# Short convolution and channel mix on one core: a rebuilt opening (weight softmax over eight partitions, mixing coefficients turned on TensorE, band matrices by thirds, load order) and a tail kept pair by pair

## The chip, the core and the metric

One core of a Trainium2 chip runs the program. Its engines work side by side and meet by semaphores: TensorE (PE; its weight loads are listed as PEld), VectorE (DVE), ScalarE (ACT), GpSimd (POOL), and SyncE (SP), which only issues transfers. PE writes to PSUM, which the kernel uses as a ring of four tiles of two banks; ACT and DVE read it. Transfers are issued by SP, ACT or POOL, and those from POOL convert fp32 to bf16 on the way. The metric is the device time of one execution in microseconds (us).

## The reference

Eight sequences of 4160 positions with 192 channels. First a causal convolution with seven taps, the taps of each of eight heads (24 channels each) being a softmax over raw weights; then a channel mix with a token shift.

```python
w = np.exp(weight - weight.max(-1, keepdims=True))      # weight: (8 heads, 7 taps)
w = w / (w.sum(-1, keepdims=True) + 1e-09)
y[b, s, h, :] = sum(w[h, k] * x_pad[b, s + k, h, :] for k in range(7))   # x_pad: 6 zeros ahead
y_prev = y one position earlier, zeros at the start
yk = mu_k * y + (1 - mu_k) * y_prev
yr = mu_r * y + (1 - mu_r) * y_prev
k = np.maximum(yk @ w_k, 0)                              # 192 -> 1024
out = 1 / (1 + np.exp(-(yr @ w_r))) * (k * k @ w_v)      # 1024 -> 192
```

## The kernel before

Two sequences are worked on together (four pairs). The tokens of a pair go through steps of 512 (256 for the first), and each step's 192-to-1024 product falls into slots of one PSUM tile; four slots are a bundle. Every slot needs six or twelve matmuls with the weights `wk`, one ReLU on ACT and one square on DVE; the product with `wv` follows some bundles later. The convolution is a matmul with a 128x128 banded matrix per head (`toe`), made once at the start. For the first eleven blocks of 120 positions (groups 0, 1 and 2 with 3, 4 and 4 blocks) it is done so that the result comes out with channels on partitions (`conv_t`); later groups go through DRAM.

The opening, which the change rebuilds, and the first bundle:

```python
    def softmax():
        nc.vector.tensor_reduce(out=w_max, in_=w_raw, axis=mybir.AxisListType.X, op=ALU.max)
        nc.vector.tensor_tensor(
            out=w_exp, in0=w_raw, in1=w_max.unsqueeze(2).to_broadcast([1, H, K]), op=ALU.subtract
        )
        nc.scalar.activation(out=w_exp, in_=w_exp, func=AF.Exp)
        nc.scalar.activation(out=w_sig, in_=w_exp[:, 0, 0:1], func=AF.Sigmoid)
        xbs[0] = three.tile([P, GB, 2, D], BF16, tag="xb", name="xb")
        for s in range(2):
            nc.scalar.copy(out=xbs[0][:, : groups[0][2], s, :], in_=x_f32[:, :, s, :])
        # then DVE: sum, reciprocal, product -> w_nrm [1, H, K]; PE: ones.T @ w_nrm -> w_bc on 128 partitions
    # ... cut ...
    def make_toe():   # for heads 0-5, then heads 6-7: w_bc * mod8 -> w_all, summed -> w_per (tap by position mod 8),
                      # then toe = w_per * band        (three DVE instructions each)
    # ... cut ...
    def prologue():
        nc.sync.dma_start(out=w_raw, ...)
        nc.vector.memset(x_f32[0:32, 0, :, :], 0.0)
        nc.vector.memset(ones_t, 1.0)
        for st in range(2):
            load_x_first(nc.scalar, 0, P, 1, groups[0][2], st, st + 1)
        load_x_first(nc.sync, 16, P, 0, 1, 0, 2)
        load_mu(0, moe_mu_k)
        load_x_first(nc.scalar, HALO, 16, 0, 1, 0, 2)
        nc.scalar.preload_act_table(AF.Exp)
        nc.vector.memset(zeros, 0.0)
        x_tile(1)
        load_x(1)
        # POOL: affine_select -> ident
        masks_band()
        load_wk()
        for i in range(SHORT):                 # 100 matmuls of one column
    # ... cut ...
        warm(warm_ps, WARM[0])
        x_tile(2)
        masks_mod8()
        softmax()
        warm(warm_ps, WARM[1])
        make_toe()
        load_x(2)
        load_mu(1, moe_mu_r)
        x_tile(3)
        load_x(3)
        load_wr()
        load_wv()
        x_tile(4)
        load_x(4)

    def bundle_first(ns):
        new_yT(0)
        tiles = [ring.tile([P, 2, BANK], FP32, tag="k", name="ps_t") for _ in range(2)]
        for n, (g, c) in enumerate((g, c) for g in range(2) for c in range(NC)):
            o = tiles[n % 2][:, n // 2 % 2, :]
            conv_t(g, c, o, range(groups[g][2]))
            to_yT(g, c, o, 0, groups[g][2], nc.scalar.copy)
            if g == 0:
                diff(0, slice(c, c + 1))
                mix(0, 0, slice(c, c + 1))
        for c in range(NC):
            for n in ns[:2]:
                k_mm(n, (c,))
        for n in ns[:2]:
            k_relu(n)
        for c in range(NC):
            diff(1, slice(c, c + 1))
            mix(1, 0, slice(c, c + 1))
        for n in ns[2:]:
            k_mm(n)
            k_relu(n)
        for n in ns:
            k_square(n)
```

`conv_t` of one channel third, the slot product and the mixing. `mu` holds the mixing coefficients with the channel on the partition:

```python
    def conv_t(g, c, o, blocks):               # both sequences of every block: 8 matmuls of 120 columns a block
    # ... cut ...
                        nc.tensor.matmul(
                            out=o[p0 : p0 + m, n * BLK : (n + 1) * BLK],
                            lhsT=xbs[g][:, i, s, c0 : c0 + m],
                            rhs=toe[:, h, 0:BLK], start=True, stop=True)
    def k_mm(n, cs=range(NC)):                 # wk columns of slots 0, 1 of step 0: first half; slots 2, 3: second half
    # ... cut ...
                    nc.tensor.matmul(out=ps[:, i, f * L : (f + 1) * L], lhsT=wk[r, c, fs], rhs=xk[r, c, :L], ...)
    def mix(s, i, sl=slice(0, NC)):            # step 0: one instruction a third; later: scale() and add_y()
    # ... cut ...
            nc.vector.scalar_tensor_tensor(out=t[:, c, :L], in0=d[:, c, :L], scalar=mu[:, i, c : c + 1],
                in1=y_of(s, sl, 0)[:, 0, :], op0=ALU.mult, op1=ALU.add)
```

From the third bundle on (`b` counts from 0), `mix_a`, `mix_b` and `mix_c` hold the mixing work that is due, `quad` is a product with `wv`, and `tr` turns group 3:

```python
    def bundle_rest(b, ns):
    # ... cut ...
        k_mm(ns[0])
        k_relu(ns[0])
        k_square(ns[0])
        if b > 2:
            run(mix_b, b)
            conv_half(units[0], 0)
        k_mm(ns[1])
        if b > 2:
            conv_half(units[0], 1)
        k_relu(ns[1])
        if b > 2:
            k_square(ns[1])
        run(rq, b)
        if quad:
            v_rows(*quad, 0)
        if b == 2:
            tr(3, 0)
            tr(3, 1)
            k_square(ns[1])
            run(mix_b, b)
        k_mm(ns[2])
        k_relu(ns[2])
        if b == 2:
            conv_half(units[0], 0)
    # ... cut ...
```

The last 64 positions of all eight sequences make one step of 256 tokens at the end; `keep_tail` stores their convolution results, and `v_last` writes the four results of 128 tokens:

```python
    y_tail = const.tile([P, NC, NPAIR // 2, TAIL + 1, 2], BF16)
    def keep_tail(p):
        c0 = YC + T0 - 1
        nc.gpsimd.tensor_copy(out=y_tail[:, :, p // 2, :, p % 2], in_=yTs[p][:, :, c0 : c0 + TAIL + 1])
    # ... cut ...
    def v_last(s, j):
    # ... cut ...
        for k in range(4):
            ps = ring.tile([P, 2, BANK], FP32, tag="k", name="ps_v")
            v_mm(ps[:, 0, 0:D], s, tile_of(s, j, k))
            nc.vector.tensor_tensor(
                out=o_sb[:, k, :],
                in0=ps[:, 0, 0:D],
                in1=r_sb[:, k // 2, k % 2 * D : (k % 2 + 1) * D],
                op=ALU.mult,
            )
            # one transfer of 128 rows for each k, by SP for k = 0, 2 and by ACT for k = 1, 3
```

## Time and profile before

| What | Value |
|---|---|
| time, median of three runs | 417.99 us (417.91 to 418.95) |
| span of the profiled execution | 416.2 us |
| PE busy | 407.2 us (98%) |
| DVE busy | 378.8 us (91%) |
| ACT busy | 347.7 us (84%) |
| POOL busy | 48.9 us (12%) |
| bytes moved by DMA | 64.59 MB, mean 155 GB/s |

Busy time is the union of an engine's instructions; a matmul's end is modelled, so a busy PE need not stream all the time. In a line of instruction groups, the columns are line and engine, operation, tiles and shapes, count, then busy us and mean ns of one, then the idle time of the engine ahead of them and what ended it. The chain of waits follows the end of the program back to whatever released each step.

### The profile page before, as it was taken

How to read it: one execution, taken by the hardware profiler on the slowest of the kernel's cores; microseconds unless marked ns; L12 is line 12 of the kernel's file. 1: busy time of each engine (PE TensorE's matmuls, PEld its weight loads, DVE VectorE, ACT ScalarE, POOL GpSimd, SP SyncE). 2: the span in 40 equal slices, each digit the busy share in tenths (PEclk: the TensorE clock that was granted, in tenths of full speed). 3: DMA queues.
4: the chain of work that ended last, by engine and by line, in shares of the span. 5: the costliest groups of instructions: out<-in, count | busy, mean ns of one | idle time of the engine just before them, and what ended most of it. 6: DMA issues, size and time to landing. Idle time of an engine off the chain costs nothing.

```text
span 416.2 us, 16358 instructions
## 1 busy us (share of the span) xinstructions
PE 407.2 (98%) x7136; PEld 316.0 (76%) x7136; DVE 378.8 (91%) x674; ACT 347.7 (84%) x408; POOL 48.9 (12%) x73
## 2 busy tenths in 40 slices
PE   6999999999999999999999999999999999999996
PEld 3667777787887778778777877877777787777895
DVE  5898799999999999999999999999999999999974
ACT  5999898898888889888988888898898788777781
POOL 6650003102030100202012010201000000000000
PEclk9999999999999999999999999999999999999999
DMA  9999779958499794959689693897936564421223
GB/s 144 193 191 178 191 185 196 224 148 160 122 196 227 166 182 120 151 164 186 175 149 204 181 183 109 146 225 148 181 95 162 139 152 125 119 69 49 77 80 115
DMA packets 134682, 64.59 MB, mean 155 GB/s; under 512 B 84926, under 2 KB 134610, under 8 KB 134610
## 3 DMA queue, kind: packets, MB, share of 16 engines
q1 hardware_dynamic: 95876, 48.28, 45.2%
q0 software_dynamic: 37872, 14.66, 30.9%
q8 instruction: 56, 0.92, 0.9%
q10 hardware_dynamic: 862, 0.61, 0.5%
q14 instruction: 16, 0.13, 0.1%
HBM read 29.89 MB, written 36.99 MB: 161 GB/s over the span
## 4 chain that ended last, share of the span: by engine, by line
PE 92%; ACT 3%; DVE 3%; issue 1%; POOL 0%; ACTq 0%; POOLq 0%
PE ps_v L577 40%; PE ps_k L492 38%; PE ps_r L549 7%; PE ps_c L310 5%; ACT k_sb L504 2%; PE ps_v L532 1%; DVE k L518 1%; ACT y L356 1%; PE warm L702 1%; DVE d L435 0%; POOL xb L126 0%; ACT yT L340 0%; DVE xk L448 0%; DVE xk L472 0%; DVE xk L466 0%
## 5 line engine op out<-in xcount | busy, mean ns | idle before, releaser
L504 ACT ACTIVATE k_sb<-ps_k 128x1024 bf16<-128x1024 f32 x260 | 260.9, 1039 | 53.2 <-PE ps_k L492 53.1
L492 PE MATMUL ps_k<-xk,wk 64*128 64x512 bf16 (+1 forms) x1632 | 200.3, 367 | 0.8 <-ACT k_sb L504 0.3
L518 DVE TENSOR_TENSOR k<-k_sb 128x1024 bf16<-128x1024 bf16 x260 | 177.7, 688 | 14.5 <-ACT k_sb L504 7.4
L577 PE MATMUL ps_v<-wv,k 64*128 64x192 bf16 x4032 | 188.8, 243 | 0.7 <-ACT k_sb L504 0.2
L577 PEld LDWEIGHTS <-k 64*128 64x128 bf16 x4032 | 172.4, 94 | 13.9 <-issue 1.5
L492 PEld LDWEIGHTS <-wk 64*128 64x128 bf16 x1632 | 87.9, 94 | 51.4 <-issue 1.1
L593 DVE TENSOR_TENSOR o_sb<-ps_v,r_sb 128x768 f32<-128x768 f32 x64 | 61.2, 957 | 11.1 <-PE ps_v L577 4.5
L557 ACT ACTIVATE r_sb<-ps_r 128x768 bf16<-128x768 f32 x65 | 54.6, 842 | 0.0
L126 POOL DMA_DIRECT2D xb<-in_x_dram x34 | 30.6, 903 | 193.1 <-PE ps_c L310 93.0
L356 ACT CAST y<-ps_c 120x960 bf16<-120x960 f32 (+4 forms) x67 | 50.7, 787 | 2.2 <-PE ps_c L310 2.1
L549 PEld LDWEIGHTS <-xr 64*128 64x128 bf16 x780 | 36.1, 94 | 11.0 <-issue 0.4
L549 PE MATMUL ps_r<-wr,xr 64*128 64x192 bf16 x780 | 43.8, 243 | 0.0
L310 PE MATMUL ps_c<-xb,toe 64*128 64x480 bf16 (+2 forms) x240 | 39.2, 335 | 0.3
L466 DVE TENSOR_SCALAR xr<-d,mu 128x512 bf16<-128x512 bf16 (+1 forms) x102 | 35.9, 355 | 0.0
L466 DVE TENSOR_SCALAR xk<-d,mu 128x512 bf16<-128x512 bf16 (+1 forms) x99 | 33.0, 361 | 0.1
L435 DVE TENSOR_TENSOR d<-yT 128x1536 bf16<-128x1536 bf16 (+3 forms) x37 | 31.3, 847 | 0.9 <-ACT yT L340 0.9
L472 DVE TENSOR_TENSOR xr<-xr,yT 128x1536 bf16<-128x1536 bf16 (+1 forms) x33 | 31.0, 938 | 1.1
L472 DVE TENSOR_TENSOR xk<-xk,yT 128x1536 bf16<-128x1536 bf16 (+2 forms) x34 | 30.5, 898 | 0.1
L310 PEld LDWEIGHTS <-toe 64*128 64x128 bf16 x240 | 13.4, 94 | 11.8 <-issue 0.9
L419 POOL COPY y_tail<-yT 128x195 bf16<-128x195 bf16 x4 | 1.7, 429 | 68.7 <-DMA yT<-y_dram 68.7
L108 POOL MEMSET xb<- 32x384 bf16 x3 | 1.2, 408 | 45.1 <-PE ps_k L492 43.8
L330 PEld LDWEIGHTS <-xb 128*32 128x32 bf16 (+3 forms) x264 | 4.3, 101 | 2.6 <-issue 1.6
(52 smaller groups left out, 61.9 us busy)
## 6 DMA issues: line engine op xcount, KB each, us to landing
out_dram<-o_sb SPq DMA_DIRECT2D x128, 192.0 KB, 2.8
y_dram<-y SPq DMA_DIRECT2D x10, 900.0 KB, 6.5
xb<-in_x_dram POOLq DMA_DIRECT2D x14, 480.0 KB, 7.9
xb<-in_x_dram POOLq DMA_DIRECT2D x6, 432.0 KB, 8.0
xb<-in_x_dram POOLq DMA_DIRECT2D x10, 192.0 KB, 5.1
y_dram<-y SPq DMA_DIRECT2D x3, 450.0 KB, 5.3
y_dram<-y SPq DMA_DIRECT2D x1, 810.0 KB, 6.0
wk<-in_moe_w_k_dram POOLq DMA_DIRECT2D x4, 192.0 KB, 6.7
```

The lines of the kernel that those rows point to most:

```text
L310: nc.tensor.matmul(out=banks[:, bank, :, :, k * G : (k + 1) * G], lhsT=toe[q, h, :], rhs=xbs[g][q, :nb, :, h * G : (h + 1) * G], start=hal ...
L356: copy(out=bass.AP(tensor=y.tensor, offset=y.offset + d0, ap=[y.ap[0], [d1 - d0, 2], [2 * D, nb], [Q, 2], [1, n]],), in_=bass.AP(tensor=ps ...
L435: nc.vector.tensor_tensor(out=shaped(s, diffs[s][:, cs, :L]), in0=y_of(s, cs, 1), in1=y_of(s, cs, 0), op=ALU.subtract)
L466: nc.vector.tensor_scalar(out=t[:, c, :L], in0=diffs[s][:, c, :L], scalar1=mu[:, i, c : c + 1], scalar2=None, op0=ALU.mult)
L472: nc.vector.tensor_tensor(out=o, in0=o, in1=y_of(s, sl, 0), op=ALU.add)
L492: nc.tensor.matmul(out=ps[:, i, f * L : (f + 1) * L], lhsT=wk[r, c, fs], rhs=xk[r, c, :L], start=c == 0 and f == 0, stop=c == NC - 1 and f ...
L504: nc.scalar.activation(out=k_sb, in_=ps.rearrange("p a b -> p (a b)"), func=AF.Relu)
L518: nc.vector.tensor_tensor(out=o, in0=i, in1=i, op=ALU.mult)
L549: nc.tensor.matmul(out=ps[:, i, k * D : (k + 1) * D], lhsT=xr[q, c, ts], rhs=wr[q, c, :], start=c == 0, stop=c == NC - 1,)
L557: nc.scalar.activation(out=r_sbs[s, j], in_=ps[:, :, 0 : 2 * D], func=AF.Sigmoid)
L577: nc.tensor.matmul(out=v_ps[s, j][:, bank, k * D : (k + 1) * D], lhsT=k2s[s][q, f, t * P : (t + 1) * P], rhs=wv[q, f, :], start=half == 0 ...
L593: nc.vector.tensor_tensor(out=o_sb.rearrange("p (b t) d -> p b (t d)", b=2), in0=v_ps.pop((s, j)), in1=r_sbs.pop((s, j)), op=ALU.mult,)
```

## The change

The opening is rebuilt so that the band matrices are there sooner. The eight heads of the softmax lie on eight partitions instead of one; Exp takes the negated maximum as its bias and gives the sum as well. Normalised weights are turned by a 32x32 DVE transpose, and eight small matmuls with shifted selection matrices (`tap8`) leave `w_per` in PSUM, in place of broadcast, mask and sum. `toe` is made in three parts, one for each third of the channels, and the copy of the first x goes by thirds too. The mixing coefficients are loaded as six rows and turned by a PE transpose, instead of a scatter of single elements. The first half of `wk` is asked for ahead of group 1 of x. In the third bundle the mixing and a square are issued ahead of the transposes. The tail is kept pair by pair instead of interleaved by two pairs, and is written by eight transfers instead of four.

```diff
-    WARM = (3, 5)
-    SHORT = 100
+    WARM = (3, 2)
+    SHORT = 95
     def load_mu(i, m):
-        for st in range(2):
-            nc.sync.dma_start(
-                out=mu[st * Q : (st + 1) * Q, i, :], in_=bass.AP(tensor=m.tensor, offset=m.offset, ap=[[1, Q], [Q, NC]])
-            )
+        nc.sync.dma_start(
+            out=mu_raw[i * NC : (i + 1) * NC, :].rearrange("c (s q) -> c s q", s=2),
+            in_=bass.AP(tensor=m.tensor, offset=m.offset, ap=[[Q, NC], [0, 2], [1, Q]]),
+        )
-    w_all = place[:, n : n + H * 8 * K].rearrange("p (h r k) -> p h r k", h=H, r=8)
-    w_raw = const.tile([1, H, K], FP32)
+    w_raw = const.tile([H, K], FP32)
-    w_nrm = const.tile([1, H, K], BF16)
-    mod8 = const.tile([P, 16], FP32)
+    w_nrm = const.tile([32, 32], BF16)
+    w_tap = const.tile([32, 32], BF16)
+    tap8 = const.tile([8, P + 8], BF16)
+    ident6 = const.tile([2 * NC, 2 * NC], FP32)
+    mu_raw = const.tile([2 * NC, P], FP32)
-    w_bc = ring.tile([P, 2, BANK], FP32, tag="k", name="w_bc")[:, 0, 0 : H * K].rearrange("p (h k) -> p h k", h=H)
-    w_per = const.tile([P, H, 8], BF16)
+    w_ps = ring.tile([P, 2, BANK], FP32, tag="k", name="w_ps")
+    w_per = w_ps[:, 0, 0 : H * 8].rearrange("p (h r) -> p h r", r=8)
-    y_tail = const.tile([P, NC, NPAIR // 2, TAIL + 1, 2], BF16)
+    y_tail = const.tile([P, NC, NPAIR, TAIL + 2], BF16)
@@ softmax, masks @@
-        nc.vector.tensor_reduce(out=w_max, in_=w_raw, axis=mybir.AxisListType.X, op=ALU.max)
-        nc.vector.tensor_tensor(
-        # ... exp of the difference, a Sigmoid on one element, copies by sequence, sum, reciprocal, product ...
+        nc.vector.tensor_reduce(out=w_max, in_=w_raw, axis=mybir.AxisListType.X, op=ALU.max, negate=True)
+        nc.scalar.activation(out=w_exp, in_=w_raw, func=AF.Exp, bias=w_max, accum_out=w_sum)
+        nc.scalar.preload_act_table(AF.Sigmoid)
         xbs[0] = three.tile([P, GB, 2, D], BF16, tag="xb", name="xb")
-        for s in range(2):
-            nc.scalar.copy(out=xbs[0][:, : groups[0][2], s, :], in_=x_f32[:, :, s, :])
-        nc.vector.tensor_reduce(out=w_sum, in_=w_exp, axis=mybir.AxisListType.X, op=ALU.add)
+        for c in range(NC):
+            cs = slice(c * Q, (c + 1) * Q)
+            nc.scalar.copy(out=xbs[0][:, : groups[0][2], :, cs], in_=x_f32[:, :, :, cs])
         nc.vector.reciprocal(out=w_sum, in_=w_sum)
-        # ... product, matmul of ones with w_nrm -> w_bc; masks_mod8: two DVE reductions of ident ...
+        nc.vector.tensor_scalar(
+            out=w_nrm[0:H, 0:K], in0=w_exp, scalar1=w_sum, scalar2=None, op0=ALU.mult
+        )
+        nc.vector.transpose(out=w_tap, in_=w_nrm)
+        for r in range(8):
+            nc.tensor.matmul(
+                out=w_per[:, :, r], lhsT=tap8[:, 8 - r : 8 - r + P], rhs=w_tap[0:8, 0:H], start=True, stop=True
+            )
+    def masks_tap():
+        nc.gpsimd.affine_select(
+            out=tap8.rearrange("p (c r) -> p c r", r=8),
+            in_=ones_t[0:8, 0:8].unsqueeze(1).to_broadcast([8, P // 8 + 1, 8]),
+        # ... one where the partition is r, else zero ...
+    def turn_mu():
+        nc.tensor.transpose(out=w_ps[:, 1, 0 : 2 * NC], in_=mu_raw, identity=ident6)
@@ make_toe @@
-        m = mod8[:, :]
-        hc = -(-2 * Q // G)
-        for h0, h1 in ((0, hc), (hc, H)):
+        for h0, h1 in ((0, 3), (3, 6), (6, H)):
-            # ... w_bc * mod8 -> w_all, reduce -> w_per ...
             nc.vector.tensor_tensor(
                 out=toe[:, h0:h1, :].rearrange("p h (c r) -> p h c r", r=8),
                 in0=w_per[:, h0:h1, :].unsqueeze(2).to_broadcast([P, n, P // 8, 8]),
                 in1=band.rearrange("p (c r) -> p c r", r=8).unsqueeze(1).to_broadcast([P, n, P // 8, 8]),
                 op=ALU.mult,
             )
+        nc.vector.tensor_copy(out=mu.rearrange("p i c -> p (i c)"), in_=w_ps[:, 1, 0 : 2 * NC])
@@ tail @@
-        nc.gpsimd.tensor_copy(out=y_tail[:, :, p // 2, :, p % 2], in_=yTs[p][:, :, c0 : c0 + TAIL + 1])
+        nc.gpsimd.tensor_copy(out=y_tail[:, :, p, 0 : TAIL + 1], in_=yTs[p][:, :, c0 : c0 + TAIL + 1])
-            return y_tail[:, cs, :, k : k + TAIL, :].rearrange("p c a t b -> p c a (t b)")
+            return y_tail[:, cs, :, k : k + TAIL]
-        return t.rearrange("p c (a t) -> p c a t", t=2 * TAIL) if s == LAST else t
+        return t.rearrange("p c (a t) -> p c a t", t=TAIL) if s == LAST else t
-            # ... v_last: one transfer for each k ...
+            for i in range(2):
+                (nc.scalar if i else nc.sync).dma_start(
+                    out=out[2 * (2 * (k % 2) + i) + k // 2, T0:S, :], in_=o_sb[i * TAIL : (i + 1) * TAIL, k, :]
+                )
@@ prologue @@
+        nc.vector.memset(ones_t, 1.0)
         nc.vector.memset(x_f32[0:32, 0, :, :], 0.0)
-        nc.vector.memset(ones_t, 1.0)
-        for st in range(2):
-            load_x_first(nc.scalar, 0, P, 1, groups[0][2], st, st + 1)
-        load_x_first(nc.sync, 16, P, 0, 1, 0, 2)
+        for st, eng in ((0, nc.scalar), (1, nc.sync)):
+            load_x_first(eng, 0, P, 1, groups[0][2], st, st + 1)
+        load_x_first(nc.scalar, 16, P, 0, 1, 0, 2)
+        load_x_first(nc.scalar, HALO, 16, 0, 1, 0, 2)
         load_mu(0, moe_mu_k)
-        load_x_first(nc.scalar, HALO, 16, 0, 1, 0, 2)
+        load_mu(1, moe_mu_r)
         nc.scalar.preload_act_table(AF.Exp)
         nc.vector.memset(zeros, 0.0)
-        x_tile(1)
-        load_x(1)
+        nc.vector.memset(w_nrm, 0.0)
         nc.gpsimd.affine_select(
         # ... ident ...
+        masks_tap()
+        load_wk(0)
+        x_tile(1)
+        load_x(1)
         masks_band()
-        load_wk()
+        load_wk(1)
+        nc.vector.tensor_copy(out=ident6, in_=ident[0 : 2 * NC, 0 : 2 * NC])
@@ later in the prologue @@
-        masks_mod8()
         softmax()
+        turn_mu()
         warm(warm_ps, WARM[1])
         make_toe()
         load_x(2)
-        load_mu(1, moe_mu_r)
@@ bundle_rest @@
         k_square(ns[0])
+        run(mix_b, b)
         if b > 2:
-            run(mix_b, b)
             conv_half(units[0], 0)
         k_mm(ns[1])
         if b > 2:
             conv_half(units[0], 1)
         k_relu(ns[1])
-        if b > 2:
-            k_square(ns[1])
+        k_square(ns[1])
         run(rq, b)
         if quad:
             v_rows(*quad, 0)
         if b == 2:
             tr(3, 0)
             tr(3, 1)
-            k_square(ns[1])
-            run(mix_b, b)
```

## The prediction

> **What bounds the kernel now.** I read the page first, then the busy time of each engine by stretch, then the opening as a timeline, then transfers and tile instructions in the stretches that mattered.
>
> The stretches, where each column is busy us and (instructions) of PE, PEld, DVE, ACT and POOL, then the granted clock, the DMA share and GB/s:
>
> ```profile
> 7.80:12.80 5.00, 4.72 (x193) 4.06 (x193) 3.88 (x13) 2.96 (x6) 2.74 (x5) 1.00 1.25 176
> 12.80:26.00 13.20, 12.12 (x239) 8.15 (x235) 11.38 (x27) 13.00 (x17) 8.25 (x12) 1.00 1.60 191
> 26.00:40.00 14.00, 13.43 (x210) 9.57 (x208) 12.94 (x24) 12.96 (x17) 1.86 (x3) 1.00 1.20 182
> 40.00:400.00 360.00, 359.78 (x6196) 280.70 (x6193) 337.22 (x584) 308.31 (x357) 29.49 (x41) 1.00 0.74 155
> 400.00:416.20 16.20, 12.37 (x209) 11.68 (x204) 9.04 (x16) 6.31 (x7) 0.00 (x0) 0.98 0.32 100
> ```
>
> From 40 to 400 us PE is busy 359.78 of 360, and the change adds or takes no instruction there. So that stretch keeps its length and only moves: everything is decided in the first 30 us and the last 5. Between 12.8 and 26 us ACT is busy 13.00 of 13.20: that stretch is ACT's. Thus what counts is how much earlier ACT's run of ReLUs begins, not how much earlier PE begins.
>
> The opening in order of time (start, length, engine, what, shapes, count, idle time before):
>
> ```profile
> 3.38 0.67 DVE L244 TENSOR_REDUCE mod<-ident 128x8 f32<-128x128 bf16 x2 [1.64 <-POOL ident L720]
> ...
> 4.42 0.25 ACT L220 ACTIVATE w_exp<-w_exp 1x56 f32<-1x56 f32 x1 [0.65 <-DVE w_exp L217]
> ...
> 5.55 2.31 PE L702 MATMUL warm<-zeros,ones_t 128*128 128x512 bf16 x5
> ...
> 6.09 1.23 ACT L225 CAST xb<-x_f 128x576 bf16<-128x576 f32 x2
> ...
> 6.82 0.56 DVE L278 TENSOR_TENSOR toe<-w_per,band 128x768 bf16<-128x768 bf16 x1
> ...
> 7.79 3.03 PE L330 MATMUL ps_t<-toe,xb 128*32 128x120 bf16 x136
> ...
> 12.85 3.77 ACT L504 ACTIVATE k_sb<-ps_k 128x1024 bf16<-128x1024 f32 x4 [0.63 <-PE ps_k L492]
> 13.29 1.53 PEld L492 LDWEIGHTS <-wk 64*128 64x128 bf16 x28 [0.44 <-DMA wk<-in_moe_w_k_dram]
> ```
>
> The reader is to see a chain through six engines: POOL first spends 1.31 to 2.95 issuing x of group 1, then makes ident (3.02 to 3.35); DVE reduces it (mod8) ahead of the softmax; Exp at 4.42; toe at 6.82 to 7.38; the first convolution at 7.79, held last by the warm-up matmuls (5.55 + 2.31 = 7.86), and by the copies of x (6.09 + 1.23 = 7.32). The first ReLU stands at 12.85.
>
> Two more answers. PE's convolution matmuls last 307 ns until 8.8 us and 216 ns from 9.7 us on, so the array ran slow and then fast; the granted-clock row doesn't show it:
>
> ```profile
> L330 PE MATMUL ps_t<-toe,xb x44: 279/307/308, 7.8 to 8.8; 128*32 128x120 bf16 x24, 128*24 128x120 bf16 x10, 128*16 128x120 bf16 x6, 128*8 128x120 bf16 x4
> L330 PE MATMUL ps_t<-toe,xb x96: 212/216/227, 9.7 to 11.4; 128*32 128x120 bf16 x48, 128*24 128x120 bf16 x16, 128*16 128x120 bf16 x16, 128*8 128x120 bf16 x16
> ```
>
> And transfers, packets, MB and share of 16 engines; the first two lines are 5 to 9 us, the last 9 to 12 us:
>
> ```profile
> q0 software_dynamic: 950, 0.49, 109.2%
> q1 hardware_dynamic: 804, 0.00, 17.8%
> ```
>
> ```profile
> q0 software_dynamic: 707, 0.59, 124.4%
> ```
>
> While the scatter of mu is under way (804 packets with next to no bytes), POOL's queue moves 0.49 / 4 = 0.122 MB per us; afterwards 0.59 / 3 = 0.197. By tile, x of group 1 (two of 192 KB) was issued at 1.3 and 2.2 us and took 5.5 and 5.8, so landed at 6.8 and 8.0; wk (four of 192 KB) was issued from 3.9 to 5.8 and took 6.2 to 7.4, so its last quarter landed at 13.2, which is the 0.44 us wait at 13.29.
>
> **What the Trainium skill says.** "TensorE: Matmul & The Clock Gate", section "What's actually happening": an idle array runs at half rate and is released by one busy window of about 3.4 us, free-running, so the moment varies. The trace agrees in kind: steady work from 5.42, fast by about 8.9. "ScalarE: Activation LUTs", "What ACT_TABLE_LOAD costs": about 1283 ns for any set; here 1.28 us for both (2.49 and 4.69 us). "DMA: Bandwidth & Descriptors", "Specifications": under 512 B a transfer isn't at line rate; the rates above agree, with 4-byte packets. "VectorE: DVE Perf Modes", "Why PSUM operands drop a tier": an fp32 PSUM operand leaves the basic rate, so toe from PSUM should cost twice as much an element as the bf16 form here; no run here shows it yet.
>
> **The change part by part.**
>
> *Up to Exp.* Removed: mod8 (0.67), the subtraction (0.20), and POOL's 1.64 us ahead of ident. Ident and tap8 come right after ones_t (which moves ahead of the memset of x_f32, from 1.47 to about 1.12): I put them at 1.25 to 1.85. The weights are tiny, and I take them as landed by 2.8. Then Exp waits for ACT's own first table load, which today runs from 2.49 to 3.77: Exp at 3.8 instead of 4.42, a gain of 0.6.
>
> *Exp to w_per.* Reciprocal, product and a 32x32 transpose, 0.2 each with 0.03 between (rows of that size take 0.19 to 0.20): 4.7. Eight tiny matmuls follow, slow array, about 0.5: w_per at 5.2. Today w_per of the first heads is there at 6.70.
>
> *Band.* POOL now issues two of wk (0.65 each) and two of x (0.77 to 0.88 each) before the band masks: 1.85 + 1.35 + 1.65 = 4.85, and 0.7 for two selects gives 5.55. Band, not w_per, should end last.
>
> *Toe by thirds.* The bf16 form took 0.56 for 768 and 0.29 for 256 elements: 0.52 ns an element over 0.155. At 1.04 ns, three heads (384) take 0.56: first third 5.6 to 6.15, second about 6.65, third 7.0, mu 7.2. The warm-up of 2 x 0.43 ends near 6.1.
>
> *Copies of x.* The second table load 4.05 to 5.3, and three copies of 384 elements, at a pitch of about 0.42 (slope from 576 in 0.66 and the ACT overlap): 5.8, 6.2, 6.6.
>
> *Convolution of group 0* thus starts at about 6.2, against 7.79: 1.6 us earlier, and ends near 8.3.
>
> *Group 1, and here the gain shrinks.* Its x now stands behind half of wk. POOL's queue can start 2.6 us after its first issue (today 1.31 to about 3.9), thus near 4.45. Without the scatter it moves about 0.19 MB per us: wk first half until 6.5, x of group 1 until 8.6, with 0.4 to the landing and 0.2 of sharing with the first x: 9.2. Today the convolution of group 1 starts at 9.75, held by the copies to yT, not by x. New start 9.2: gain 0.55. PE then idles from 8.3 to 9.2.
>
> *To the first ReLU.* Today 9.75 to 12.85 is 3.1 us (three convolutions with their copies, then 24 matmuls in 1.3). The same distance gives 12.3. The second half of wk lands near 11.3 and so no longer holds PE, which reaches it at about 12.3. DVE's chain for step 1, today 11.31, starts at 10.4 and isn't the bound. ACT then runs through its 13 us block: the gain of 0.55 is carried to 26 us, and by PE to the end.
>
> *Third bundle.* The same DVE instructions, two scalings (0.35) and a square (0.69) ahead of a copy (0.34): under 0.2 either way.
>
> *Tail.* The last DVE product ended at 412.77, its transfer landed 2.0 later. Half-size transfers on two queues: 0 to 0.2 us earlier; four more completions to wait for at the end, at 0.06 each: 0 to 0.25 later. Net 0. The tail's DVE and POOL work has slack (DVE 9.04 of 16.2).
>
> Sum: -0.55, so 417.99 - 0.55 = 417.44, said as 417.4.
>
> **The rivals.**
>
> 1. *The whole 1.6 us arrives.* It would need x of group 1 by 8.2 us. For it: the scatter's 804 packets are gone, and wk's rows are 1 KB packets. Against: 768 KB have to pass ahead of it at 0.19 MB per us. Time 416.4.
> 2. *The new order costs all.* If the queue stays at 0.122 MB per us, or POOL starts later, group 1 lands at 10.2 or after; ReLU at 13.3; time 418.4.
> 3. *The array stays slow longer.* PE now has two pauses, 3.5 to 4.7 and 8.3 to 9.2, and fewer warm-up matmuls. If no window is busy enough, group 1 and the first slots run slow: three convolutions (5.0 us of matmul for 264 in all, thus some 0.15 more each) and 1.3 for the slots: up to 1.5 later; time 418.9. I give this a quarter in part, and it's why my range reaches above the old median.
> 4. *Transfers late in the kernel change.* Eight smaller stores in place of four could only touch the last 2 us.
>
> **Range and chances.** All branches lie between 416.4 and 418.9; 2% is 8.4 us, more than the whole opening can give (PE begins at 7.8) and more than any delay here. 80% range 416.5 to 418.4. Faster by over 2%: 0.01, within 0.98, slower 0.01.
>
> **What would show it.** Exp near 3.8, toe's first third near 5.6 at about 0.56 us, and the first convolution near 6.2. Group 1's convolution at 9.2 right when x lands, with PE idle before it; the first ReLU at 12.3; the matmul of 120 columns at 216 ns, not 307, by then. From 40 us on all the same, shifted by half a microsecond. It is wrong if ReLUs start after 12.85, if ACT shows gaps between 12 and 26 us, or if the stretch from 40 us on is longer.

## The result and the profile after

| | before | after |
|---|---|---|
| median time | 418.06 us (417.91 to 418.95, 4 runs) | 423.58 us (422.87 to 423.93, 4 runs) |
| ratio to before, 95% interval | | 1.0125 [1.0106, 1.0145] |
| span of the profiled execution | 416.2 us | 421.9 us |
| first ReLU starts | 12.85 us | 16.61 us |
| last DVE result starts | 412.41 us | 417.20 us |

The changed kernel is 1.25% slower, and above the predicted range (416.5 to 418.4). The view by stretches says where the 5.7 us of span went (columns as in the prediction: the stretch, its length, then busy us and instructions of PE, PEld, DVE, ACT and POOL, then the granted clock, DMA share and GB/s):

```profile
7.80:12.80 5.00, 2.68 (x105) 1.99 (x98) 2.79 (x10) 1.93 (x4) 3.01 (x5) 1.00 1.40 188
12.80:26.00 13.20, 12.06 (x249) 8.04 (x250) 9.62 (x21) 10.36 (x14) 5.99 (x9) 0.87 1.47 173
26.00:40.00 14.00, 12.55 (x205) 9.12 (x201) 12.66 (x26) 12.54 (x17) 3.91 (x6) 1.00 1.23 159
40.00:400.00 360.00, 359.63 (x6174) 280.70 (x6171) 336.97 (x581) 308.07 (x359) 29.71 (x41) 1.00 0.74 156
400.00:421.90 21.90, 17.16 (x299) 15.71 (x294) 13.03 (x26) 10.72 (x12) 0.00 (x0) 1.00 0.31 92
```

From 40 to 400 us PE is as full as before (359.63 against 359.78): that stretch only moved. In 7.8 to 12.8 us PE has 2.68 us of work where it had 4.72, and in 12.8 to 26 us ACT is busy 10.36 where it had 13.00 and the granted clock is 0.87 where it was 1.00. From 26 to 40 us PE loses 0.88. So there are three places: the opening, the third bundle, and the last microseconds.

The opening of the changed kernel in order of time:

```profile
3.86 0.30 ACT L216 ACTIVATE w_exp<-w_raw,w_max 8x7 f32<-8x7 f32 x1
...
6.06 1.34 ACT L221 CAST xb<-x_f 128x384 bf16<-128x384 f32 x3 [0.51 <-DMA x_f<-in_x_dram]
...
6.27 0.24 PE L245 MATMUL w_ps<-ident,mu_raw 6*128 6x6 f32 x1 [0.92 <-DMA mu_raw<-in_moe_mu_r_dram]
...
6.63 1.35 DVE L259 TENSOR_TENSOR toe<-w_ps,band 128x384 bf16<-128x384 f32 x3 [1.69 <-PE w_ps L245]
...
7.41 2.14 PE L311 MATMUL ps_t<-toe,xb 128*32 128x120 bf16 x72
...
11.22 0.70 PE L311 MATMUL ps_t<-toe,xb 128*32 128x120 bf16 x39 [0.85 <-DMA xb<-in_x_dram]
...
12.92 1.59 PE L311 MATMUL ps_t<-toe,xb 128*32 128x120 bf16 x55 [0.99 <-issue]
...
14.44 1.89 PE L473 MATMUL ps_k<-xk,wk 64*128 64x256 bf16 x16
```

The early part came: Exp is at 3.86, and the first convolution starts at 7.41 against 7.79. The loss begins at group 1. PE ends group 0 at 9.55 and then waits for `xb` until 11.22 (two matmuls at 10.14 with the part that came first), and after 41 matmuls it stops once more for 0.99 us with the word "issue": it waits for nothing that another engine or a transfer of data releases. Then the array runs slow. In the view of the tile, and in the view by stretches:

```profile
L311 PE MATMUL ps_t<-toe,xb x55: 258/305/308, 12.9 to 14.2; 128*32 128x120 bf16 x27, 128*8 128x120 bf16 x14, 128*16 128x120 bf16 x8, 128*24 128x120 bf16 x6
```

```profile
12.83:16.24 3.41, 3.32 (x73) 2.59 (x74) 2.62 (x8) 1.12 (x2) 2.58 (x4) 0.50 1.57 186
```

305 ns is the slow figure of the prediction (307 against 216), and this time the granted clock shows it: 0.50 from 12.83 to 16.24.

What was the "issue"? The transfers of each queue (packets, MB, share of 16 engines) hold a queue that the prediction passed over: q8 brings PE's own instructions. In 5 to 9 us of the kernel before:

```profile
q8 instruction: 1, 0.02, 1.5%
```

In 5 to 9 us of the changed kernel there is none:

```profile
q0 software_dynamic: 1017, 0.56, 114.1%
q10 hardware_dynamic: 3, 0.00, 0.1%
q1 hardware_dynamic: 2, 0.00, 0.0%
```

It comes in 9 to 13 us:

```profile
q0 software_dynamic: 1424, 0.77, 139.6%
q8 instruction: 1, 0.02, 1.5%
```

In the records of single transfers this 16 KB transfer begins at 5.38 in the kernel before and at 10.52 here; PE goes on at 12.92, which is 2.40 later. Below, "instructions begin" means the start of this transfer. That it is what PE waits for rests on two regularities over the runs below. In each of the eight executions with such a pause, PE goes on 2.2 to 2.45 us after the start of the transfer, whether the pause is 0.34 or 4.22 us long. And the pause falls at the same count: by the records of the trace, after 444 to 446 weight loads and matmuls. The Trainium skill, "Runtime: NRT & Kernel Launch", section "Instruction fetch mechanics", says that an engine gets its instructions in blocks of 16 KiB (256 of them) through a DMA queue of its own, and that the cost of passing a block's end is mostly hidden. The trace agrees with the size (each transfer of this queue is 16384 bytes) and not with "hidden": PE stood still for 0.99 us here.

**The third bundle.** The shift of the ReLUs (how much later each one starts than the same one in the kernel before) is +3.76 up to the eleventh and +4.74 from the twelfth on. Two lines of the waits of the changed kernel, 26 to 44 us (engine and line that waited, who ended it: us in total, times, longest):

```profile
ACT y L337 <- PE ps_c L291: 1.9, 2, 1.4
...
PE ps_c L291 <- DVE yT L391: 0.8, 1, 0.8
```

`yT L391` is the copy by `tr` that turns group 3. Before, no wait of PE for it is listed in this stretch. It now stands on DVE behind two scalings of the mixing and the square, and starts at 30.83 instead of 25.84, which is 1.24 more than the shift up to there; the next convolution on PE wants the PSUM tile that it frees.

**The end.** The timeline of the last results, before:

```profile
411.48 1.87 ACTq L619 DMA_DIRECT2D out_dram<-o_sb  x2
411.74 1.35 SPq L619 DMA_DIRECT2D out_dram<-o_sb  x2
...
412.41 0.36 DVE L613 TENSOR_TENSOR o_sb<-ps_v,r_sb 128x192 f32<-128x192 f32 x1 [0.30 <-PE ps_v L532]
```

and after:

```profile
415.81 2.52 ACTq L601 DMA_DIRECT2D out_dram<-o_sb  x4
...
416.58 2.70 SPq L601 DMA_DIRECT2D out_dram<-o_sb  x4
417.20 0.36 DVE L594 TENSOR_TENSOR o_sb<-ps_v,r_sb 128x192 f32<-128x192 f32 x1 [0.30 <-PE ps_v L513]
```

The last result ends at 417.56, but SP is in the row of its four issues until 416.58 + 2.70 = 419.28 (0.56 to 0.65 each, end to end). Before, its two were done at 413.09. From the start of the last DVE result to the span's end it was 3.8 us and is 4.7. The last issue starts 0.39 us after that result's start before (at 412.80, on ACT) and 1.52 after it now (at 418.72, on SP); from there to the end it is 3.4 and 3.2 us. So the time goes into the issues, and not into slower landing.

Sum of the three: 3.76 + 0.98 + 0.9 = 5.6 of the 5.7 us.

### The profile page after: what moved, and what is told of

It reads as the page before. It is cut to its first block, busy times and chain, and to the rows that moved or that the text cites. A ratio compares the mean times of both kernels' runs of the same rounds, so it can differ in the third digit from the quotient of the medians.

```text
span 421.9 us, 16365 instructions
## 1 busy us (share of the span) xinstructions
PE 408.3 (97%) x7136; PEld 317.7 (75%) x7136; DVE 377.9 (90%) x671; ACT 347.9 (82%) x409; POOL 49.4 (12%) x74
## 4 chain that ended last, share of the span: by engine, by line
PE 89%; ACT 2%; issue 1%; DVE 0%; ACTq 0%
PE ps_v L558 39%; PE ps_k L473 37%; PE ps_r L530 7%; PE ps_c L291 4%; ACT k_sb L485 1%; PE ps_v L513 1%; ACT y L337 0%; DVE o_sb L574 0%; DVE o_sb L594 0%; ACTq L337 0%; ACTq L299 0%
## 5 line engine op out<-in xcount | busy, mean ns | idle before, releaser
L291 PEld LDWEIGHTS <-toe 64*128 64x128 bf16 x240 | 13.6, 94 | 12.9 <-issue 2.0
L311 PE MATMUL ps_t<-toe,xb 128*32 128x120 bf16 (+3 forms) x264 | 6.5, 259 | 2.8 <-DMA xb<-in_x_dram 1.4
```

The source lines that it names most:

```text
L291: nc.tensor.matmul(out=banks[:, bank, :, :, k * G : (k + 1) * G], lhsT=toe[q, h, :], rhs=xbs[g][q, :nb, :, h * G : (h + 1) * G], start=hal ...
```

## The experiments

Times stand against the kernel before on the same chip in the same session, so the ratio is what compares, with its 95% interval in brackets. Each profile shows one execution of several, and the executions of one kernel differ by up to 3 us (the old spread of the first x below: 418.15 to 421.35).

### One part undone at a time

First the load order alone: all of `wk` after x of group 1, and nothing else undone.

```diff
-        load_wk(0)
         x_tile(1)
         load_x(1)
         masks_band()
-        load_wk(1)
+        load_wk(0, 1)
```

Expected:

> The changed kernel with one thing undone: x of group 1 is issued ahead of all of wk. Theory (the order delays x of group 1, and PE's pauses while it waits let the clock fall): x of group 1 lands near 9.0 instead of 11.2, the first ReLU near 12.5 instead of 16.6, and the time falls by about 4.0, to some 419.4. Rival (the opening is late for another reason: the slow start of POOL's queue, or PE waiting for its own instructions between 11.9 and 12.9): the first ReLU stays after 15 and the time falls by less than 1.5.

Measured: 422.45 us, 1.0095 [1.0074, 1.0115]; first ReLU 15.22. x of group 1 landed at 8.13 instead of 11.18, as hoped for, and yet most of the loss stayed. The timeline of PE:

```profile
6.83 3.21 PE L311 MATMUL ps_t<-toe,xb 128*32 128x120 bf16 x113
11.79 1.59 PE L311 MATMUL ps_t<-toe,xb 128*32 128x120 bf16 x55 [1.75 <-issue]
13.31 4.72 PE L473 MATMUL ps_k<-xk,wk 64*128 64x256 bf16 x60
```

PE no longer waits for data, and stops at the very same place: 113 = 72 of group 0 + 41 of group 1, and 55 are left. It waits 1.75 us for its instructions (they begin at 9.55). The wait had been half hidden behind the one for x.

Then the third bundle in its old order, and the tail in its old layout with four stores:

```diff
-        run(mix_b, b)
         if b > 2:
+            run(mix_b, b)
         # ... cut ...
-        k_square(ns[1])
+        if b > 2:
+            k_square(ns[1])
         # ... cut: b == 2, behind the transposes ...
+            k_square(ns[1])
+            run(mix_b, b)
```

Expected:

> The changed kernel with the third bundle in its old order. Theory (the copy of the transposed group 3 waits on DVE behind two scalings and a square, and the next convolution waits for its PSUM tile): the shift against the kernel before no longer grows from 3.75 to 4.74 in the third bundle, the idle 0.8 of PE is gone, the time falls by 1.0 to about 422.5. Rival (the growth comes from transfers, only at the same moment): no change.

Measured: 422.73, 1.0099 [1.0077, 1.0121]. The shift is +4.31 from the first ReLU on and does not grow. In the waits from 26 to 44 us the line `PE ps_c <- DVE yT` is gone, and the other one reads:

```profile
ACT y L337 <- PE ps_c L291: 0.9, 2, 0.6
```

```diff
-    y_tail = const.tile([P, NC, NPAIR, TAIL + 2], BF16)
+    y_tail = const.tile([P, NC, NPAIR // 2, TAIL + 1, 2], BF16)
         # ... cut: what writes and reads y_tail follows it ...
-            for i in range(2): (nc.scalar if i else nc.sync).dma_start(...)   # 64 rows each
+            (nc.scalar if k % 2 else nc.sync).dma_start(...)                  # 128 rows
```

Expected:

> The changed kernel with the old tail: layout interleaved, four transfers instead of eight. Theory (each transfer costs about 0.6 of SP's sequencer, so SP's four in a row end 1.3 later than the last result): the distance from the last DVE instruction to the end falls from 4.7 to 3.8, the time by 0.9 to about 422.6. Rival (stores of 64 rows land later): the same total, but SP's issues would not be in a row; told apart by the profile.

Measured: 421.88, 1.0077 [1.0057, 1.0096]. From the start of the last DVE result (415.42) to the end it is 3.4 us instead of 4.7. The first ReLU stood at 14.61 in this run and at 17.16 in the one with the old third bundle, though both openings are that of the changed kernel (16.61): x of group 1 landed at 10.4, 12.9 and 11.2, in this order. So a single undoing measures its part only roughly. All three diffs together, expected:

> The changed kernel with all three undone; the softmax on eight partitions, toe by thirds from PSUM, the turned mixing coefficients and the shorter warm-up stay. If the three losses add up (4.0, 1.0, 0.9), it takes 423.6 - 5.9 = 417.7, near the kernel before at 418.0. If the rebuilt opening is worth what its own chain gains and x no longer holds it, down to 417.2. If the opening is late for another reason than the order, 421 or more.

Measured: 420.10, 1.0041 [1.0022, 1.006]; first ReLU 14.86, x landed at 8.37, instructions begin at 9.86, PE stood 2.30 us until 12.13. So the three parts don't hold the whole loss: the late instructions belong to something else.

### Is it the number of warm-up matmuls?

The theory: with 8 warm-up matmuls fewer, the end of a block of instructions falls on another matmul, one that is at once followed by a wait. First, SHORT at 105 in the kernel with the three parts undone, which moves every later matmul ten places on; then the kernel before with the new counts (95 and 2).

```diff
-    SHORT = 95
+    SHORT = 105     # with the three diffs above
```

Expected:

> All three undone, and 105 instead of 95 short warm-up matmuls. Seen in the four runs so far: PE stops at the same instruction each time (41 matmuls into group 1), and goes on 2.2 to 2.4 us after a 16 KB instruction transfer begins, at 9.5 to 10.5; in the kernel before that first transfer begins at 5.4. Theory (the transfer is asked for when PE's stream passes a fixed place; with 95 that place lies behind the wait for the softmax, with 105 ahead of it, as with 100 and three more before): the transfer begins by 5.5, the pause of 2.3 is gone, the first ReLU comes at 12.6 to 13.2 instead of 14.9, the time falls by 1.5 to 2 against 420.1. Rival (the transfer is merely held back by the other transfers, wherever the place lies): it begins after 9 again, and the time stays.

```diff
-    WARM = (3, 5)
-    SHORT = 100
+    WARM = (3, 2)
+    SHORT = 95      # nothing else changed in the kernel before
```

Expected:

> The kernel before with nothing but the warm-up counts of the changed one: 95 short matmuls instead of 100, and 3 and 2 instead of 3 and 5 long ones. Theory (the place where the instruction transfer is asked for moves behind a wait): the first instruction transfer begins after 8 instead of 5.4, PE pauses for 1 to 2.3 in group 1, and the kernel is 1 to 2 slower, near 420. Rival (the counts only fill idle time): 418, as before.

Measured with SHORT at 105: 420.85, 1.006 [1.0035, 1.0085], first ReLU 15.92, instructions begin at 9.39, a pause of 2.2 us. Measured for the kernel before with the new counts: 418.61, 1.0005 [0.9992, 1.0018], first ReLU 12.86, instructions begin at 4.97, no pause. The new counts do no harm to the old kernel, and more warm-up doesn't mend the new one. This theory of why the transfer is late fell. But the pause itself moved as the end of a block of instructions would: with ten more warm-up matmuls ahead, PE stops ten convolution matmuls sooner (103 in place of 113):

```profile
6.58 2.94 PE L311 MATMUL ps_t<-toe,xb 128*32 128x120 bf16 x103
11.73 1.90 PE L311 MATMUL ps_t<-toe,xb 128*16 128x120 bf16 x65 [2.21 <-issue]
```

Two more with SHORT at 105: the changed kernel with the third bundle and the tail undone but the new order kept, and the changed kernel alone:

Expected of the first:

> The changed kernel with 105 short matmuls, old third bundle and old tail, and the new order kept: half of wk ahead of x of group 1. Against the run with all three undone and 105 this differs in the order alone. Theory: x lands at 10.3 to 11.2 instead of 8.4, PE idles for 1 to 2 there, the first ReLU comes 1 to 2 later, the time is 1 to 1.5 higher. Rival (wk is then what ends last in the other order, so the order is neutral): within 0.5.

Expected of the second:

> The changed kernel with nothing altered but 105 instead of 95 short matmuls. Theory: the pause of 1.0 for instructions goes, and less of the slow clock; 1.0 to 2.5 faster than 423.6, that is 421 to 422.6. Rival: no change, as x still lands at 11.2 and PE waits for it anyway.

Measured: 420.99, 1.0063 [1.0041, 1.0085], with x landing at 11.68 and instructions beginning at 9.45; and 423.0, 1.0106 [1.0084, 1.0129], with 11.06 and 9.38. In neither does PE pause for instructions, which begin late all the same: x lands so late that they are there when PE gets to that place (by about 11.8, if they take the 2.2 to 2.45 us of the other runs). The changed kernel with 105 is still at 423.0, so where x is late the pause for instructions adds little (1.0106 without it, 1.0125 with it). The pair is of use otherwise, too: they differ in the third bundle and the tail alone, by 0.43%, 1.8 us.

### Which part of the opening delays the instructions?

From the kernel with the three parts undone, one more part was undone in each of four: x of group 1 issued by POOL ahead of the masks; the memset of ones behind that of the first x; `mu` loaded by the old scatter, with no turn on PE; the first x spread over the queues as before.

POOL's x ahead of the masks:

```diff
+        x_tile(1)
+        load_x(1)
         # selects for ident and tap8
-        x_tile(1)
-        load_x(1)
```

> All three undone, and POOL issues x of group 1 ahead of the masks, as in the kernel before. Open: why the first 16 KB instruction transfer of PE begins at 9.4 to 10.5 here and at 5 in the kernel before. If it is the moment at which POOL's queue gets its first work (1.3 against 1.76): the transfer begins near 5, PE's pause of 2.3 in group 1 is gone, the time is 418 to 419. If not: begins after 9 again, 420.

Ones late:

```diff
-        nc.vector.memset(ones_t, 1.0)
         nc.vector.memset(x_f32[0:32, 0, :, :], 0.0)
+        nc.vector.memset(ones_t, 1.0)
```

> All three undone, and the memset of the ones after that of x, as in the kernel before: the short matmuls begin at 1.5 instead of 1.1, and PE passes the place of the request 0.4 later. If the moment of the request decides: the transfer begins near 5 and the pause is gone, 418 to 419. If not: after 9, 420.

The old scatter of `mu`:

```diff
-        nc.sync.dma_start(out=mu_raw[...], in_=bass.AP(..., ap=[[Q, NC], [0, 2], [1, Q]]))
+        for st in range(2):
+            nc.sync.dma_start(out=mu[st * Q : (st + 1) * Q, i, :], in_=bass.AP(..., ap=[[1, Q], [Q, NC]]))
-        load_mu(1, moe_mu_r)
-        turn_mu()
+        load_mu(1, moe_mu_r)                   # behind load_x(2) again
-        nc.vector.tensor_copy(out=mu.rearrange("p i c -> p (i c)"), in_=w_ps[:, 1, 0 : 2 * NC])
```

> All three undone, and the mixing coefficients loaded by the old scatter of single elements, with no turn on PE. If the many small packets let the instruction transfer in between (or its rows of 256 bytes held it): begins near 5, pause gone, but the first mixing may then wait for the coefficients until about 9; 418 to 419.5. If not: after 9, 420.

The old spread of the first x:

```diff
-        for st, eng in ((0, nc.scalar), (1, nc.sync)):
-            load_x_first(eng, 0, P, 1, groups[0][2], st, st + 1)
-        load_x_first(nc.scalar, 16, P, 0, 1, 0, 2)
+        for st in range(2):
+            load_x_first(nc.scalar, 0, P, 1, groups[0][2], st, st + 1)
+        load_x_first(nc.sync, 16, P, 0, 1, 0, 2)
         # ... cut: load_mu(0) ahead of the 16 halo rows again ...
```

> All three undone, and the first x spread over the queues as in the kernel before (two thirds on ACT, block 0 on SP). If a long transfer on SP's queue held the instruction transfer: begins near 5, pause gone, 418 to 419. If not: after 9, 420.

| undone besides the three | time us | ratio [95%] | instructions begin | PE's pause | first ReLU |
|---|---|---|---|---|---|
| POOL's x first | 421.90 | 1.0074 [1.0046, 1.0102] | 12.56 | 4.22 | 18.37 |
| ones late | 418.64 | 1.0011 [0.9998, 1.0024] | 4.01 | none | 12.90 |
| old scatter of mu | 418.20 | 0.9990 [0.9980, 1.0001] | 4.51 | none | 12.15 |
| old spread of first x | 419.79 | 1.0034 [1.0020, 1.0048] | 8.90 | 1.49 | 15.22 |

Two of the four bring the instructions back to 4 to 4.5 us, and each of them alone is enough. With the ones late PE's timeline has no pause:

```profile
6.74 4.37 PE L311 MATMUL ps_t<-toe,xb 128*24 128x120 bf16 x164
```

With POOL's x first it stays, at the same 113th matmul. The profile is of the slowest of seven executions (423.34), so 4.22 is not typical, and the interval of the ratio overlaps that of the kernel with three parts undone (1.0022 to 1.006):

```profile
15.00 1.59 PE L311 MATMUL ps_t<-toe,xb 128*32 128x120 bf16 x55 [4.22 <-issue]
```

The opening with the old scatter:

```profile
4.96 0.36 PE L228 MATMUL w_ps<-w_tap,tap 8*128 8x8 bf16 x8 [1.53 <-DVE w_tap L226]
...
5.44 1.35 DVE L259 TENSOR_TENSOR toe<-w_ps,band 128x384 bf16<-128x384 f32 x3 [0.53 <-PE w_ps L228]
...
6.22 2.04 PE L310 MATMUL ps_t<-toe,xb 128*32 128x120 bf16 x68
```

```profile
12.15 4.69 ACT L484 ACTIVATE k_sb<-ps_k 128x1024 bf16<-128x1024 f32 x5 [1.23 <-PE ps_k L472]
```

These are the times that were predicted (toe 5.6, convolution 6.2, ReLU 12.3), but in a kernel with x of group 1 first and the old `mu`; its third bundle and tail are old, too. The profile is of one of its fastest executions (417.61, median 418.20).

### The order and the instructions, each by itself

Three kernels turn the finding round: the changed kernel with only the scatter of `mu` put back; the same opening with the third bundle and the tail old as well (it differs from the kernel with the old scatter above in the load order alone); and the kernel before with nothing but the turned `mu` and the early ones. A fourth is the kernel before with the new third bundle and the new tail.

The changed kernel with the diff of `mu` above, expected:

> The changed kernel with one thing undone: the mixing coefficients come by the old scatter and aren't turned on PE. Third bundle, tail and order are the changed ones. Theory (the late instruction transfer is what the opening loses most by, and it is late only with the turned load): the transfer begins before 5.5; what is left is x of group 1 landing late and the two known losses of 0.98 and 0.9: the first ReLU at 12.9 to 14, the time 420.5 to 421.5. Rival (order alone loses the opening): the first ReLU after 15, time 423.

The kernel with the old scatter, and the new order on top of it:

```diff
+        load_wk(0)
         x_tile(1)
         load_x(1)
         masks_band()
-        load_wk(0, 1)
+        load_wk(1)
```

Expected:

> Old third bundle, old tail, old scatter of the mixing coefficients, and the changed order (half of wk ahead of x). It differs from the run at 418.2 in the order alone, and should have no pause for instructions. Theory (the order costs when nothing else waits): x lands at 9.5 to 10.5 instead of 8.2, the first ReLU at 13.3 to 14.0 instead of 12.15, the time 419.3 to 420. Rival (wk is what ends last in the other order, so the order is neutral): within 0.4 of 418.2.

The kernel before with the diff of `mu` and that of the ones turned round (rows loaded and turned by PE beside `w_bc`, ones first), expected:

> The kernel before with two things of the change: the turned load of the mixing coefficients, and the ones made first. Theory (these two together make the first instruction transfer late, whatever the rest): it begins after 8.5 instead of 5.4, PE pauses 1 to 2.5 in group 1, the time is 419.5 to 421. Rival (it needs the rest of the new opening as well): begins before 5.5, 418.

The kernel before with the diffs of the third bundle and of the tail turned round, expected:

> The kernel before with the new third bundle and the new tail. Theory: the ReLU shift grows by 0.98 in the third bundle, and the end comes 0.9 later after the last result; 418.3 + 1.9 = 420.2. Rival (the losses only show together with the late opening): less than 1.

The changed kernel with the scatter back: 423.75, 1.0137 [1.0113, 1.016]: no gain, though its instructions begin at 4.09. What was called the rival came true, with the first ReLU at 16.16. The other wait is still there: x of group 1 lands at 11.20 and PE stands 1.78 + 0.73 us for it:

```profile
10.23 0.29 PE L310 MATMUL ps_t<-toe,xb 128*32 128x120 bf16 x2 [1.78 <-DMA xb<-in_x_dram]
11.25 2.62 PE L310 MATMUL ps_t<-toe,xb 128*32 128x120 bf16 x94 [0.73 <-DMA xb<-in_x_dram]
```

The order alone: 421.99, 1.0092 [1.0077, 1.0107], against 418.20 and 0.9990. So the order by itself costs 1.0%, about 4.2 us, more than twice what was expected. PE's timeline:

```profile
6.73 1.67 PE L310 MATMUL ps_t<-toe,xb 128*24 128x120 bf16 x52
10.73 0.28 PE L310 MATMUL ps_t<-toe,xb 128*32 128x120 bf16 x2 [2.33 <-DMA xb<-in_x_dram]
11.79 2.63 PE L310 MATMUL ps_t<-toe,xb 128*32 128x120 bf16 x94 [0.78 <-DMA xb<-in_x_dram]
14.35 3.94 PE L472 MATMUL ps_k<-xk,wk 64*128 64x256 bf16 x58
```

No "issue" here; the waits are for data. The 94 matmuls last 2.63 us because the array is slow (a median of 307 ns, where the kernel at 418.2 had 216 from 8.8 us on). The first ReLU is at 15.66.

The kernel before with turned `mu` and early ones: 419.81, 1.0042 [1.0020, 1.0064]; instructions begin at 9.40 instead of 5.38, and a pause of 0.34 appears at the 113th matmul:

```profile
8.59 2.85 PE L333 MATMUL ps_t<-toe,xb 128*32 128x120 bf16 x113
11.78 0.92 PE L333 MATMUL ps_t<-toe,xb 128*32 128x120 bf16 x55 [0.34 <-issue]
```

The two edits bring about the late instructions in the old kernel, too. The profile is of the fastest of six executions (418.62), so how long PE pauses at the median of 419.81 isn't shown. Part of the loss is the turn itself: PE waits for the rows of `mu`, so the warm-up behind it, and then the convolution, start later (8.59 against 7.79).

The kernel before with the new third bundle and tail: 420.01, 1.0042 [1.0028, 1.0057]: +1.0 in the third bundle, with the wait of PE that the changed kernel has, and +0.8 at the end:

```profile
PE ps_c L310 <- DVE yT L410: 0.8, 1, 0.8
```

The pairs above give as much (1.0106 against 1.0063; 1.0137 against 1.0092).

### Two tries to do better

The kernel with the old scatter, with x of group 1 issued by POOL ahead of the masks:

```diff
+        x_tile(1)
+        load_x(1)
+        masks_tap()
+        masks_band()
+        load_wk(0, 1)
         # select for ident, now last; the copy to ident6 goes
-        masks_tap()
-        x_tile(1)
-        load_x(1)
-        masks_band()
-        load_wk(0, 1)
```

Expected:

> What the runs leave as good: the softmax on eight partitions and toe by thirds, old scatter, old third bundle, old tail, x of group 1 ahead of wk; and POOL issues x before any mask, the mask for the transposes last. Against the run at 418.2: POOL's queue starts at 1.3 instead of 1.76, so x and wk land up to 0.4 earlier, the first ReLU at 11.8 to 12.1, the time 417.6 to 418.0 where the kernel before takes 418.3. Rival (the queue is full anyway): equal to 418.2; or the instruction transfer comes late again: 420.

Measured: 418.45, 1.0010 [0.9998, 1.0021]. The first ReLU is at 12.41 (0.44 earlier than before), but the lead is gone after the eleventh ReLU: from there on the shift is +0.20. No gain.

And the kernel with the old scatter and the new pair-by-pair tail, with one store of 128 rows for each result, to tell the layout from the number of stores:

```diff
-                    ap=[[D, TAIL], [2 * S * D, 2], [1, D]],
+                    ap=[[2 * S * D, 2], [D, TAIL], [1, D]],
```

Expected:

> The run at 418.2 with the tail kept pair by pair, as in the changed kernel, but written by four transfers of 128 rows instead of eight of 64. Theory (the loss of 0.9 at the end is the number of transfers on SP's sequencer, not the layout): within 0.2 of 418.2, and the end 3.7 to 3.8 after the last result. Rival (the layout is slower to read or write): 0.5 or more slower.

Measured: 425.57, 1.0181 [1.0167, 1.0194]. The first ReLU is 0.20 earlier than before and the last result, at 412.22, 0.19, so the layout costs nothing up to there. But the span ends at 423.3, 11.1 us after the start of that result. The transfers of this kernel from 411 to 423.5 us, in 40 slices:

```profile
DMA  0499951111111111111111111111111111100000
GB/s 0 155 297 339 324 153 15 37 32 25 37 44 49 22 44 49 44 49 44 49 44 49 44 49 44 44 49 44 49 44 49 44 49 44 49 10 0 0 0 0
```

The stores crawl at 44 to 49 GB/s, with a tenth of the engines busy, where the store ahead of them ran at over 300. The Trainium skill, "DMA: Bandwidth & Descriptors", section "Why a DMA increments its semaphore by 16 and not by 1", says that a transfer is spread over the largest number of engines, up to 16, that divides the slowest dimension of both sides; here this is 2 on the side of the output. The trace agrees with that: from 414 to 421.5 us 0.13 of the 16 engines' time is busy, and 2 of 16 are 0.125. For the question that the run was made for, four stores or eight, it says nothing: a new loss of some 7 us (11.1 against 3.8) covers it.

## Why the prediction was wrong

**"Up to Exp", "Exp to w_per", "Band": right.** Exp 3.86 (3.8), `w_per` 5.35 (5.2), band 5.38 (5.55).

**"Toe by thirds": size right, start missed by 1.0 us.** 384 elements took 0.552 us (0.56); with 0.414 for 256 that is 0.138 / 128 = 1.08 ns an element from PSUM, twice the 0.52 of the bf16 form. The copies of x were late as well (6.06 for 5.3, at the end a wait of 0.51 for the transfer), but toe came later still. The turn of `mu` had been left out of the path. Its result lies in the same PSUM tile as `w_per`, and toe waited 1.69 us for PE's `w_ps` of the turn (6.27), which waited for the rows of `mu`. With the scatter back toe starts at 5.44 and the convolution at 6.22: the sum was right for a kernel without the turn.

**"Group 1": the step that failed first.** It had x landed at 9.2: 0.79 MB at 0.19 MB per us from 4.45 on, until 8.6, and 0.6 more for the landing and for sharing. x landed at 11.18. Both terms were too small. First the rate. The scatter was taken for the cause of the slow early rate, because the two lay side by side in time. The changed kernel has none, and from 4.45 to 9 us its queue moved 0.63 MB, 0.14 per us; from 5 to 9 it was 0.56 MB, and 0.52 with the scatter back. So the prediction's rates are no sign of what the 4-byte packets cost POOL's queue. Only from 9 on it was 0.77 / 4 = 0.19. So 0.79 MB had passed at 9.7 and not at 8.6. Then the rest: x was complete 1.5 us later and not 0.6, when the queue had moved 1.08 MB. Some 0.29 MB of what was issued behind x had gone in between. Rival 2 (10.2 or after) had the mechanism, and put it at 418.4, because it carried the delay of x and nothing else. The order alone cost about 4.2 us.

**"To the first ReLU", 3.1 us: held only for an undisturbed PE.** From x of group 1 at 11.18 to the ReLU at 16.61 it was 5.4. Of this, 0.99 is the wait for instructions, and then the slow array: 55 convolution matmuls at 305 ns and slots at a median of 418 ns where a fast array took 269. Rival 3 named the slow array, put it at 1.5 and gave it a quarter. It was no chance apart from the rest, but the wait for x isn't what lets the clock fall: after that wait the array still ran at 216 ns (from 11.22), and it fell only at the end of the pause for instructions (12.83). The kernel with three parts undone, which never waited for x, has a granted clock of 0.50 in 14 to 16 us after its pause of 2.30. With the load order alone undone the matmuls behind the pause are slow, too (a median of 308 ns from 11.79 to 13.3), though the clock row stands at 1.00 there. What exactly makes it fall isn't shown.

**Not foreseen: PE's own instructions.** No rival had them. Two waits lay over each other, for x until 11.22 and for instructions until 12.92, so that undoing one alone gave 1.1 us (order; the intervals 1.0106 to 1.0145 and 1.0074 to 1.0115 overlap) or nothing (scatter of `mu`). With the third bundle and the tail old:

| | x of group 1 first | half of wk first |
|---|---|---|
| scatter of mu (instructions from 4.0 to 4.5) | 418.20, 0.9990 | 421.99, 1.0092 |
| turned mu (instructions from 9.4 to 9.9) | 420.10, 1.0041 | 420.99, 1.0063 (SHORT 105) |

The losses don't add: 0.51% by the turned `mu` and 1.02% by the order apart, 0.73% together (the intervals of the last two overlap).

That the instructions come late when the turned `mu` and the early ones meet is shown in both directions: in the eleven kernels with both they began at 8.9 to 12.6 us, and in the nine that lacked one or both at 4.0 to 5.5. Why these two delay the transfer is open, and so is which part of the turned `mu` does it (the load by rows, the earlier load of `mu_r` or the transpose on PE), as they were only undone together. It is not the count of warm-up matmuls, not the place of POOL's first issue and not the spread of the first x; each was tried.

**"Third bundle", under 0.2: it was +0.98.** The step counted the DVE instructions ahead of the copy (scalings of 0.35 and a square of 0.69) and then took it that nothing waits for the copy, which starts 1.24 later. PE does, for the PSUM tile.

**"Tail", net 0: it was +0.9.** The step priced four more completions at 0.06 each, and not four more issues at 0.55 to 0.65 on two sequencers that work them off one by one. Over all runs the old tail ends 3.4 to 3.9 after the start of the last result, and the new one 4.6 to 4.75. That it is the number of stores is read from the timeline; a kernel with the new layout and fewer fast stores wasn't measured.

**Right: a shift at 26 us is carried to the end unchanged,** 4.74 at the twelfth ReLU and 4.79 at the last result. From 40 us on nothing is longer, as predicted, while two of the prediction's signs of being wrong came: ReLUs after 12.85, and gaps of ACT (10.36 us busy of 13.2). In one profile the gain of 0.55 is there: with the order, `mu`, third bundle and tail undone the first ReLU is 0.70 earlier and the last result 0.53. The median time is then 0.9990 [0.9980, 1.0001], not told apart from the kernel before. No version here is clearly faster than it.

## What to carry to other kernels

Put first on a slow queue what the next busy engine needs first, and take the queue's rate from the same stretch of the profile, not from a later one. When a tensor engine's idle time is put down to "issue", look at the queue that brings its instructions; and when undoing the suspected part gives little, look for a second wait under the first and undo both. At a kernel's end count the issues on each queue one by one, and the dimension that a store is split on.

## What the runs showed of the hardware that was not expected

- PE's instruction transfers of 16 KB can hold it up: from the transfer's start to PE's next matmul it took 2.2 to 2.45 us with POOL's queue full (9.55 to 11.79, 9.86 to 12.13, 9.39 to 11.73, 8.90 to 11.35, 10.52 to 12.92, 12.56 to 15.00), and PE stood for up to 4.22 us.
- In the changed kernel the granted clock was 0.50 from 12.83 to 16.24, 3.41 us, after waits of PE of 0.59, 0.85 and 0.99 us, although PE was busy for 3.32 of it. The clock row doesn't show every slow stretch: in other profiles matmuls of 305 to 308 ns stand beside a row at 1.00.
- POOL's queue moves 0.12 to 0.14 MB per us from 5 to 9 us and 0.17 to 0.19 from 9 to 13; a scatter of 804 packets beside it makes at most the difference between 0.12 and 0.14. Why it begins slow is open. Transfers of this queue overlap: the second 192 KB of x landed only when 0.29 MB issued later had moved, too.
- One issue takes 0.55 to 0.65 us on SP and on ACT at the end of the kernel; the same bytes in eight stores of the new layout instead of four of the old end 0.9 us later.
- The same 128 rows stored with an outermost dimension of 2 on the output's side kept the transfers busy for about 9.5 us after the last result; with 64 they landed 2.0 us after it.
